# x2 computed token-major in 512-column matmuls and transposed, the last x2 blocks behind the last h, the expert operands in seven tiles built in small pieces

## Chip, cores and metric

The kernel runs on one core of a Trainium2 chip. The metric is the device time of one execution in microseconds (us): the median of several runs.

## The reference

Three layers, one behind the other, on 1536 tokens of 512 values. All arithmetic is float32.

```python
# 1: causal attention in a window of 128, plus 4 sink tokens (2 x 8 heads x 768 x 64)
a = softmax(where(is_sink | in_window, q @ k.T / 8, -1e9)); x = (a @ v) as (1536, 512)
# 2: SoLU layer
h = x @ w_in                                   # 512 -> 1024
solu = h * softmax(h)
ln = (solu - mean) / sqrt(var + 1e-6) * g_ln
x2 = ln @ w_out                                # 1024 -> 512
# 3: 8 experts, all of them for all tokens, weighted by a Sinkhorn-normalised gate
P = exp(x2 @ w_gate - max); 8 times: rows to 1, columns to 1, times N / E
for e in range(8): out += P[:, e] * (relu(x2 @ w1[e]) @ w2[e])
```

## The kernel before

Every float32 product is made of three matmuls on operands split into a high and a low part (`mm3`: high x high, high x low, low x high). A `split` takes one ScalarE copy (high) and one subtract (low), on VectorE from PSUM, or both on GpSimd for weights.

The tokens form T = 12 blocks of 128. A main loop in `fast_path` runs over slots `s`, one for each block and head (NS = 96), and over some more slots until its queues are empty. A slot emits the scores and softmax of one head, the transposes and the a @ v product of earlier heads, the steps of a layer norm that are due (`later`, a table by slot), and then, by `bulk`, a budget of matmuls from a queue: 1.0 us a slot in the first half, 1.3 behind it. The queue holds two kinds of units, written as generators that yield an assumed cost at every matmul:

- `h_unit(t)`: 24 matmuls of 512 columns give h of a block in PSUM (`hp`); behind it come, two to eight slots later, the maximum (L235), exp (L238), the product with its sum (L241), the squares (L249), the norm (L256 and, on GpSimd, L257), and then two groups of four transposes (L268), whose results are split into `lt`. These transposes wait in `tr_q` and are popped at heads 3 and 7, and one a slot behind the last head.
- `x2_unit(p)`: x2 of a pair of blocks, feature-major. The weights `w_out` are the stationary operand, `lt` of the two blocks is the moving one (256 columns): 2 x 48 matmuls into one PSUM bank each (tag `mm`, one buffer). A bank is copied to `x2f` by ScalarE (L310), or, where the pair crosses a boundary of 384 tokens, half by ScalarE (L312) and half by VectorE (L313).

The pairs 0 to 3 are queued with a delay of 28 slots. Pairs 4 and 5 are queued when everything else is done (behind slot NS + 6), after the attention's memory has been closed; then `Experts.begin` is emitted.

The experts take the tokens in four parts of 384 columns, two parts at a time (n = 0, 1), and use seven products instead of eight for each 2 x 2 block product. `build_x(n)` makes the seven operands from `x2f` (X11, X21, X22 and the differences T1 to T4) into one tile of seven parts, 128 x 768 elements a step: a copy on ScalarE (L644), a subtract on VectorE (L645), the differences on VectorE or GpSimd (L649). `begin` builds n = 0; n = 1 is built at the second unit of the experts. The weights of a slice are loaded on SP's queue, combined (L684 to L687) and split (L76, L80) by GpSimd. `Experts.run` goes through 64 units (32 slices x 2), each `first` (7 products of 6 matmuls of 384 columns, L716, with the relu split on L728 and L729) beside `second` of the unit before (36 matmuls of 512 columns). The gate's logits and the Sinkhorn steps go between the products.

The order of instructions on each engine is fixed when the program is built, by a list scheduler that simulates the engines: it takes what is ready in the order of emission, corrected by `high_priority(offset)`, by which instructions move that far forward. Each engine then works through its queue in that order. Memory of a closed pool is used again, and a tile waits for the tiles that lay in its place.

Of the kernel before, what the change touches and what calls it, by code (L numbers as in the profile page):

```python
# [15 lines left out]
P = 128  # L16
# [5 lines left out]
def tile_sink_attention__then__solu_moe__then__sinkhorn_moe(  # L22
# [175 lines left out]
    ln = {}  # L198
# [20 lines left out]
    def h_unit(t, xt, pp, later, tr_q):  # L219

        hp = pp["h"].tile([P, F], F32, name="hp", tag="h")
# [37 lines left out]
        if t % 2 == 0:  # L259
            ln[t // 2] = pp["lnT"].tile([P, 2, KF, 2, P], F32R, name="lt", tag="lt", bufs=2)  # L260
        lt = ln[t // 2]

        def s_tr(g):
# [7 lines left out]
            def post(ps):  # L271
                fs = slice(g * 4, g * 4 + 4)
                split_psum(lt[:, 0, fs, t % 2], lt[:, 1, fs, t % 2], ps)
# [18 lines left out]
    def x2_unit(p, pp):  # L292

        lt = ln.pop(p)
        for b in {2 * p // 3, (2 * p + 1) // 3} - set(x2f):
            x2f[b] = xa_tile(b, [P, KD, NX])
        for d2 in range(KD // 2):
            ps = pp["mm"].tile([P, 2, 2 * P], F32, name="x2p", tag="mm")
            for dd in range(2):
                for f in range(KF):  # L300
                    c0 = (f % 2) * DM + (2 * d2 + dd) * P
                    wt = wout_t[f // 2][:, :, c0:c0 + P]
                    rh, rl = (lt[:, i, f].rearrange("p a b -> p (a b)") for i in range(2))
                    for _ in mm3(ps[:, dd], wt[:, 0], wt[:, 1], rh, rl, f == 0, f == KF - 1):
                        yield 0.109
            ds = slice(2 * d2, 2 * d2 + 2)
            t = 2 * p
            if t % 3 < 2:
                c = t % 3 * P
                nc.scalar.activation(out=x2f[t // 3][:, ds, c:c + 2 * P], in_=ps, func=ACTF.Copy)  # L310
            else:
                nc.scalar.activation(out=x2f[t // 3][:, ds, 2 * P:], in_=ps[:, :, 0:P], func=ACTF.Copy)  # L312
                nc.vector.tensor_copy(x2f[t // 3 + 1][:, ds, 0:P], ps[:, :, P:])  # L313
# [302 lines left out]
    class Experts:  # L616
# [20 lines left out]
        def build_x(self, n, tp):  # L637

            x = self.x[n] = self.xp[n].tile([P, 7, 2, 2, NX], F32R, name=f"x{n}")
# [3 lines left out]
            def put(k, src):  # L643
                nc.scalar.activation(out=x[:, k, 0], in_=src, func=ACTF.Copy)  # L644
                nc.vector.tensor_tensor(out=x[:, k, 1], in0=src, in1=f32(x[:, k, 0]), op=ALU.subtract)  # L645

            def minus(e, z, a, b):
                t = tp(z)
                e.tensor_tensor(out=t, in0=a, in1=b, op=ALU.subtract)  # L649
                return t  # L650

            t3 = minus(nc.gpsimd, 0, b22, b12)
            t1 = minus(nc.vector, 1, b12, b11)
            put(self.X11, b11)
            put(self.T3, t3)
            put(self.X21, b21)
            t2 = minus(nc.vector, 0, b22, t1)
            put(self.T1, t1)
            t4 = minus(nc.gpsimd, 1, b21, t2)
            put(self.T2, t2)  # L660
            put(self.T4, t4)
            put(self.X22, b22)

        def temp(self, tag):
            if tag == "h1":
                return f32(self.hp.tile([P, 2, 2, NX], F32R, name="h1", tag="h1", bufs=2))[:, 0]
            return self.wf.tile([P, 2, NX], F32, name=tag, tag=tag)
# [37 lines left out]
        def seed(self):  # L705

            x = self.x[0][:, 0, 0, 0]
# [3 lines left out]
        def product(self, ps, w, k, x, kx, start):  # L711
            for kk in range(2):
                wh, wl = w[:, 0, k, kk], w[:, 1, k, kk]
                xh, xl = x[:, kx, 0, kk], x[:, kx, 1, kk]
# [75 lines left out]
        def x_parts(self, b):  # L790

            x = self.x[b // 2]
            if b % 2 == 0:
                return x[:, self.X11], x[:, self.X21]
# [93 lines left out]
    def fast_path(stack):  # L888
# [62 lines left out]
        def beside():  # L951

            return tc.high_priority(offset=0)
# [244 lines left out]
```

## Time and profile before

| | |
|---|---|
| median of 3 runs | 1362.11 us (1360.24 to 1362.42) |
| the profiled execution, its own time | 1362.57 us |
| its span, first to last instruction | 1360.5 us |
| mean granted TensorE clock | 0.982 |
| TensorE busy | 1317.5 us (97%) |
| VectorE, GpSimd, ScalarE busy | 708.2, 541.9, 373.4 us |
| chain that ended last | TensorE 89%, VectorE 4% |

Engines are called PE (TensorE), PEld (its weight loads), DVE (VectorE), ACT (ScalarE), POOL (GpSimd) and SP. The granted clock is given as a share: 1.0 is 2.4 GHz, 0.5 is 1.2 GHz. Matmuls overlap, so that the distance of two starts, and not the duration of one, is what a matmul costs in a full queue.

### The profile page before, as it was taken

How to read it: one execution, taken by the hardware profiler on the slowest of the kernel's cores; microseconds unless marked ns; L12 is line 12 of the kernel's file. 1: busy time of each engine (PE TensorE's matmuls, PEld its weight loads, DVE VectorE, ACT ScalarE, POOL GpSimd, SP SyncE). 2: the span in 40 equal slices, each digit the busy share in tenths (PEclk: the TensorE clock that was granted, in tenths of full speed). 3: DMA queues.
4: the chain of work that ended last, by engine and by line, in shares of the span. 5: the costliest groups of instructions: out<-in, count | busy, mean ns of one | idle time of the engine just before them, and what ended most of it. 6: DMA issues, size and time to landing. Idle time of an engine off the chain costs nothing.

```text
span 1360.5 us, 17867 instructions
## 1 busy us (share of the span) xinstructions
PE 1317.5 (97%) x6993; PEld 1171.5 (86%) x6993; DVE 708.2 (52%) x1352; ACT 373.4 (27%) x837; POOL 541.9 (40%) x560
## 2 busy tenths in 40 slices
PE   6799999987999999999999999999999999999998
PEld 5678888886789898989999999989999989999986
DVE  7976554544657454444444444544444544444544
ACT  5666454632422111111111111111111111111111
POOL 7862111243733643444333334444343333334410
PEclk9779999997999999999999999999999999999999
DMA  7411211001101111101111111111111001101102
GB/s 219 136 50 32 47 32 24 9 17 31 47 20 43 32 32 43 36 31 47 32 31 32 32 31 31 32 33 45 32 39 40 32 32 31 32 31 32 32 1 96
DMA packets 86287, 56.38 MB, mean 41 GB/s; under 512 B 41520, under 2 KB 74288, under 8 KB 86192
## 3 DMA queue, kind: packets, MB, share of 16 engines
q1 hardware_dynamic: 86192, 55.13, 13.8%
q8 instruction: 57, 0.93, 0.3%
q14 instruction: 38, 0.31, 0.1%
HBM read 51.97 MB, written 3.15 MB: 41 GB/s over the span
## 4 chain that ended last, share of the span: by engine, by line
PE 89%; DVE 4%; ACT 1%; issue 1%; POOL 0%; DVEq 0%; POOLq 0%; ACTq 0%
PE pb L716 15%; PE p L87 13%; PE p L85 13%; PE p L83 13%; PE pa L716 10%; PE pd L716 5%; PE pz L716 5%; PE av L522 2%; PE x2p L83 2%; PE x2p L85 2%; PE x2p L87 1%; PE hp L87 1%; PE hp L83 1%; PE hp L85 1%; DVE x L645 1%; PE trp L494 1%
## 5 line engine op out<-in xcount | busy, mean ns | idle before, releaser
L783 DVE SCALAR_TENSOR_TENSOR xa<-p,pr,xa 128x512 f32<-128x512 f32 x348 | 250.7, 748 | 207.0 <-PE p L87 207.0
L85 PE MATMUL p<-w,h 128*128 128x512 f32 x768 | 301.3, 392 | 0.0
L83 PE MATMUL p<-w,h 128*128 128x512 f32 x768 | 300.1, 391 | 0.5 <-DVE xa L783 0.5
L87 PE MATMUL p<-w,h 128*128 128x512 f32 x768 | 282.0, 394 | 2.1 <-DVE h L729 2.1
L716 PE MATMUL pb<-x,w 128*128 128x384 f32 x1152 | 234.0, 338 | 0.0
L76 POOL TENSOR_SCALAR w<-wf 128x1792 fp32r<-128x1792 f32 x32 | 54.3, 1697 | 437.2 <-PE pb L716 437.0
L716 PEld LDWEIGHTS pb<-x,w 128*128 128x128 f32 x1152 | 206.0, 188 | 5.7
L87 PEld LDWEIGHTS p<-w,h 128*128 128x128 f32 x768 | 143.6, 188 | 28.7 <-DVE h L729 2.5
L716 PE MATMUL pa<-x,w 128*128 128x384 f32 x768 | 167.1, 340 | 0.2 <-DVE h L729 0.2
L83 PEld LDWEIGHTS p<-w,h 128*128 128x128 f32 x768 | 144.2, 188 | 25.4 <-issue 0.9
L85 PEld LDWEIGHTS p<-w,h 128*128 128x128 f32 x768 | 144.2, 188 | 21.5
L728 ACT ACTIVATE h<-pz 128x384 fp32r<-128x384 f32 x64 | 31.4, 491 | 449.1 <-DVE pz L750 449.1
L716 PEld LDWEIGHTS pa<-x,w 128*128 128x128 f32 x768 | 139.2, 189 | 13.8 <-DVE h L729 0.5
L80 POOL TENSOR_TENSOR w<-wf,w 128x512 fp32r<-128x512 f32 (+1 forms) x128 | 148.3, 1191 | 2.6
L729 DVE SCALAR_TENSOR_TENSOR h<-pb,h 128x384 fp32r<-128x384 f32 x64 | 35.6, 557 | 159.5 <-ACT h L728 159.5
L80 POOL TENSOR_TENSOR w<-wr,w 128x512 fp32r<-128x512 f32 x64 | 83.7, 1330 | 0.2
L728 ACT ACTIVATE h<-pb 128x384 fp32r<-128x384 f32 x64 | 31.5, 492 | 179.1 <-PE pb L716 179.1
L716 PE MATMUL pz<-x,w 128*128 128x384 f32 x384 | 78.0, 338 | 0.0
L716 PE MATMUL pd<-x,w 128*128 128x384 f32 x384 | 77.9, 337 | 0.0
L750 DVE TENSOR_TENSOR pz<-pb,z 128x384 f32<-128x384 f32 x64 | 36.3, 566 | 76.6 <-PE pb L716 76.6
L716 PEld LDWEIGHTS pz<-x,w 128*128 128x128 f32 x384 | 69.2, 188 | 5.3
L83 PE MATMUL x2p<-lt,w 128*128 128x256 f32 x192 | 58.1, 303 | 10.1 <-DVE xa L313 8.9
(203 smaller groups left out, 1899.8 us busy)
## 6 DMA issues: line engine op xcount, KB each, us to landing
wf<-in_moe_w_dram SPq DMA_DIRECT2D x128, 128.0 KB, 2.3
wr<-in_moe_w_dram SPq DMA_DIRECT2D x32, 512.0 KB, 3.5
raw<-in_moe_w_in_dram SPq DMA_DIRECT2D x8, 512.0 KB, 5.9
raw<-in_moe_w_out_dram SPq DMA_DIRECT2D x8, 512.0 KB, 3.6
qk<-in_q_dram SPq DMA_DIRECT2D x12, 256.0 KB, 2.9
qk<-in_k_dram SPq DMA_DIRECT2D x12, 256.0 KB, 2.7
v<-in_v_dram SPq DMA_DIRECT2D x12, 256.0 KB, 2.8
out_dram<-xa SPq DMA_DIRECT2D x12, 256.0 KB, 3.5
```

The costliest lines, as they stand in the source:

```text
L76: nc.gpsimd.tensor_scalar(hi, src, 1.0, 0.0, ALU.mult, ALU.add)
L80: nc.gpsimd.tensor_tensor(lo[:, cs], src[:, cs], f32(hi[:, cs]), ALU.subtract)
L83: nc.tensor.matmul(ps, lhsT=lh, rhs=rh, start=start, stop=False)
L85: nc.tensor.matmul(ps, lhsT=lh, rhs=rl, start=False, stop=False)
L87: nc.tensor.matmul(ps, lhsT=ll, rhs=rh, start=False, stop=stop)
L494: nc.tensor.transpose(ps[:, hh, z], a[:, o:o + P], ident)
L522: nc.tensor.matmul(self.av_ps[:, h], lhsT=at[:, hh, z], rhs=self.raw["v", tv][:, h], start=h == 0 and n == 0, stop=h == H - 1 and n == len ...
L716: nc.tensor.matmul(ps, lhsT=a, rhs=b, start=start and kk == 0 and z == 0, stop=kk == 1 and z == 2, skip_group_check=True,)
L728: nc.scalar.activation(out=h[j][:, f, 0], in_=ps, func=ACTF.Relu)
L729: nc.vector.scalar_tensor_tensor(out=h[j][:, f, 1], in0=ps, scalar=0.0, in1=f32(h[j][:, f, 0]), op0=ALU.max, op1=ALU.subtract)
L750: nc.vector.tensor_tensor(out=pz, in0=pb, in1=z, op=ALU.add)
L783: nc.vector.scalar_tensor_tensor(out=acc, in0=ps, scalar=self.pr[:, t, e:e + 1], in1=acc, op0=ALU.mult, op1=ALU.add)
```

## The change

`x2_unit` now takes one block of 128 tokens, token-major: `lt` is the stationary operand and `w_out` the moving one, 24 matmuls of 512 columns into one bank. ScalarE copies the bank to a staging tile `xs` (one buffer), four TensorE transposes (through `tr_q`, popped at heads 1, 3 and 7) bring it to the feature-major form, and ScalarE copies that to `x2f`. `lt` is a tile per block (four buffers) instead of one per pair (two). A unit may start when its `lt` is written.

The last h unit has PSUM banks of its own (`h2`), and a second bank `mm2` is opened for x2, both in place of the attention's banks. The units of blocks 8 to 11 are queued as soon as the queue has nothing ready behind the last h; from there `begin` is emitted in pieces, two a slot. `beside` moves the slot's own instructions forward by 200 from slot NS - 2 on.

The seven operands of the experts are tiles of their own, and `build_x` is a generator of 22 pieces of 128 x 384 elements; those of n = 1 are emitted two a step in the first two units. The temporary that lay in an h tile is in the pool `lp`. The loop that the general path runs is changed to fit; it isn't executed here.

```diff
-    def h_unit(t, xt, pp, later, tr_q):
+    def h_unit(t, xt, pp, later, tr_q, tag="h"):
-        hp = pp["h"].tile([P, F], F32, name="hp", tag="h")
+        hp = pp[tag].tile([P, F], F32, name="hp", tag=tag)
...
-        if t % 2 == 0:
-            ln[t // 2] = pp["lnT"].tile([P, 2, KF, 2, P], F32R, name="lt", tag="lt", bufs=2)
-        lt = ln[t // 2]
+        lt = pp["lnT"].tile([P, 2, KF, P], F32R, name="lt", tag="lt", bufs=4)
...
+                if g == 1:
+                    ln[t] = lt
...
+    def x2_unit(t, pp, tr_q, tag="mm"):
+        lt = ln.pop(t)
+        b, c = divmod(t, 3)
+        if b not in x2f:
             x2f[b] = xa_tile(b, [P, KD, NX])
+        ps = pp[tag].tile([P, DM], F32, name="x2p", tag=tag)
+        for f in range(KF):
+            cs = slice(f % 2 * DM, f % 2 * DM + DM)
+            wt = wout_t[f // 2]
+            for _ in mm3(ps, lt[:, 0, f], lt[:, 1, f], wt[:, 0, cs], wt[:, 1, cs], f == 0, f == KF - 1):
+                yield 0.227
+        xs = pp["lnT"].tile([P, DM], F32, name="x2s", tag="x2s")
+        nc.scalar.activation(out=xs, in_=ps, func=ACTF.Copy)
+
+        def pe():
+            ps = pp["tr"].tile([P, KD, P], F32, name="trp", tag="tr")
+            for j in range(KD):
+                nc.tensor.transpose(ps[:, j], xs[:, j * P:(j + 1) * P], ident)
+            return ps
+
+        def post(ps):
+            nc.scalar.activation(out=x2f[b][:, :, c * P:(c + 1) * P], in_=ps, func=ACTF.Copy)
+
+        tr_q.append((pe, post))
...
-            x = self.x[n] = self.xp[n].tile([P, 7, 2, 2, NX], F32R, name=f"x{n}")
+            x = self.x[n] = [None] * 7
+            for k in (self.X11, self.T3, self.T1, self.T2, self.X22, self.T4, self.X21):
+                x[k] = self.xp[n].tile([P, 2, 2, NX], F32R, name=f"x{n}_{k}", tag=f"x{n}_{k}")
...
             def put(k, src):
+                for a in range(2):
+                    nc.scalar.activation(out=x[k][:, 0, a], in_=src[:, a], func=ACTF.Copy)
+                    nc.vector.tensor_tensor(
+                        out=x[k][:, 1, a], in0=src[:, a], in1=f32(x[k][:, 0, a]), op=ALU.subtract
+                    )
+                    yield
+            def minus(e, t, a, b):
+                for z in range(2):
+                    e.tensor_tensor(out=t[:, z], in0=a[:, z], in1=b[:, z], op=ALU.subtract)
+                    yield
...
+            build = self.build_x(1, lambda z: self.temp(("tt", "tx")[z]))
             for u, (s, n) in enumerate(units):
-                if u == 1:
-                    self.build_x(1, lambda z: self.temp(("tt", "h1")[z]))
-                if u < 2:
+                if u == 0:
                     step_side()
                     step_side()
...
+                    if u < 2:
+                        next(build, None)
+                        next(build, None)
...
         def begin(self):
-            self.build_x(0, lambda z: self.temp(("tt", "wr")[z]))
             self.load_w1(0)
+            build = self.build_x(0, lambda z: self.temp(("tt", "wr")[z]))
+            for _ in range(4):
+                next(build)
+                yield
             self.split_w1(0)
+            for _ in build:
+                yield
             self.load_w1(1)
             self.load_w2(0)
...
-            return tc.high_priority(offset=0)
+            return tc.high_priority(offset=0 if s < NS - 2 else 200)
+
+        def put_x2(t, tag="mm"):
+            queue.append((lambda: xa and t in ln, x2_unit(t, pp, tr_q, tag)))
...
-                elif tr_q and (h in (3, 7) or s >= NS):
+                elif tr_q and (h in (1, 3, 7) or s >= NS):
...
+                    if tt == T - 1:
+                        psum_a.close()
+                        for nm in ("h", "mm"):
+                            pp[nm + "2"] = pool(psum_b, f"ps_{nm}2", space=PS)
+                    queue.insert(0, (lambda: True, h_unit(tt, fast.x.pop(tt), pp, later, tr_q, "h2" if tt == T - 1 else "h")))
+                    if tt < T - 4:
+                        put_x2(tt)
...
-            if att_open and s > NS + 6 and not queue:
-                att_open = False
+            if begin is None and s > LX + NS - H and not any(x[2:] or x[0]() for x in queue):
                 att.close()
                 ex.open_early(stack)
-                psum_a.close()
-                queue.append((s, x2_unit(T // 2 - 2, pp)))
-                queue.append((s + 10, x2_unit(T // 2 - 1, pp)))
-        ex.begin()
+                for tt in range(T - 4, T):
+                    put_x2(tt, "mm" if tt % 2 else "mm2")
+                begin = ex.begin()
+            if begin:
+                next(begin, None)
+                next(begin, None)
```

## Rows read from the trace of the kernel before

**Rows 1.** Busy time by stretches: us, each engine's busy us (count), granted clock, DMA.

```profile
100.00:300.00 200.00, 199.21 (x1404) 171.67 (x1403) 99.99 (x296) 99.89 (x256) 37.76 (x54) 1.00 0.12 27
300.00:338.00 38.00, 25.39 (x169) 24.11 (x168) 19.59 (x25) 11.00 (x18) 16.51 (x12) 0.82 0.09 28
338.00:377.00 39.00, 36.72 (x192) 31.07 (x191) 23.73 (x26) 17.85 (x34) 26.69 (x17) 0.96 0.14 41
377.00:1345.00 968.00, 967.81 (x4832) 874.22 (x4831) 477.52 (x809) 178.85 (x378) 383.02 (x368) 1.00 0.11 34
```

**Rows 2.** Timeline of TensorE, x2's end: start, us, line, out<-in, count [idle before <-releaser].

```profile
311.42 0.58 PE L83 MATMUL x2p<-lt,w 128*128 128x256 f32 x1 [8.86 <-DVE xa L313]
...
317.13 0.34 PE L87 MATMUL x2p<-lt,w 128*128 128x256 f32 x1
...
322.43 1.09 PE L268 MATMUL trp<-ident,u 128*128 128x128 f32 x8 [2.47 <-POOL u L257]
323.77 0.38 PE L83 MATMUL x2p<-lt,w 128*128 128x256 f32 x1 [0.25 <-ACT lt L67]
324.50 0.58 PE L85 MATMUL x2p<-lt,w 128*128 128x256 f32 x1 [0.34 <-DVE lt L68]
...
327.44 0.31 PE L87 MATMUL x2p<-lt,w 128*128 128x256 f32 x1
...
332.35 0.39 PE L83 MATMUL x2p<-lt,w 128*128 128x256 f32 x1 [0.69 <-ACT xa L310]
...
338.03 0.28 PE L87 MATMUL x2p<-lt,w 128*128 128x256 f32 x1
```

**Rows 3.** Timeline of VectorE, then of ScalarE, in the same stretch.

```profile
303.28 5.35 DVE L645 TENSOR_TENSOR x<-xa,x 128x768 fp32r<-128x768 f32 x3
...
309.75 1.21 DVE L241 CUSTOM_DVE_ANT_0 u<-hp,u 128x1024 f32<-128x1024 f32 x1
...
310.96 0.41 DVE L313 COPY xa<-x2p 128x256 f32<-128x256 f32 x1
...
319.23 0.95 DVE L645 TENSOR_TENSOR x<-wr,x 128x768 fp32r<-128x768 f32 x1
...
313.20 1.12 ACT L249 ACTIVATE hp<-u,st 128x1024 f32<-128x1024 f32 x1 [5.90 <-DVE st L244]
...
331.70 0.60 ACT L310 ACTIVATE xa<-x2p 128x512 f32<-128x512 f32 x1 [7.49 <-PE x2p L87]
```

**Rows 4.** Timelines: last h matmuls of blocks 10, 11; their u on GpSimd.

```profile
282.67 0.39 PE L87 MATMUL hp<-w,xt 128*128 128x512 f32 x1
...
300.70 0.39 PE L87 MATMUL hp<-w,xt 128*128 128x512 f32 x1
...
292.16 2.39 POOL L257 TENSOR_TENSOR u<-u,gains 128x1024 f32<-128x1024 f32 x1 [1.21 <-DVE u L256]
...
319.45 2.92 POOL L257 TENSOR_TENSOR u<-u,gains 128x1024 f32<-128x1024 f32 x1 [0.69 <-DVE u L256]
```

**Rows 5.** Timelines of TensorE, VectorE and GpSimd, start of the experts.

```profile
350.84 0.50 PE L87 MATMUL p<-w,h 128*128 128x512 f32 x1 [2.12 <-DVE h L729]
...
341.84 6.54 DVE L645 TENSOR_TENSOR x<-xa,x 128x768 fp32r<-128x768 f32 x3
...
347.52 6.58 POOL L80 TENSOR_TENSOR w<-wf,w 128x512 fp32r<-128x512 f32 x4
```

**Rows 6.** Timeline of TensorE: one h unit; transposes.

```profile
70.34 0.47 PE L83 MATMUL hp<-w,xt 128*128 128x512 f32 x1
...
75.67 0.39 PE L87 MATMUL hp<-w,xt 128*128 128x512 f32 x1
...
102.15 0.66 PE L268 MATMUL trp<-ident,u 128*128 128x128 f32 x4
...
291.34 0.60 PE L324 MATMUL trp<-ident,xs 128*128 128x128 f32 x4
291.70 0.36 PE L83 MATMUL x2p<-lt,w 128*128 128x256 f32 x1
```

More of the change, by code (lines that the diff above doesn't have):

```diff
@@ L643, in put @@
             def put(k, src):
[L644 to L662, printed above, removed]
+                for a in range(2):
[8 more added lines that the diff above has]
+                    yield
+            t3, t1 = tp(0), tp(1)
+            yield from minus(nc.gpsimd, t3, b22, b12)
+            yield from put(self.X11, b11)
+            yield from minus(nc.vector, t1, b12, b11)
+            yield from put(self.T3, t3)
+            yield from put(self.X21, b21)
+            t2 = tp(0)
+            yield from minus(nc.vector, t2, b22, t1)
+            yield from put(self.T1, t1)
+            yield from put(self.T2, t2)
+            t4 = tp(1)
+            yield from minus(nc.gpsimd, t4, b21, t2)
+            yield from put(self.X22, b22)
+            yield from put(self.T4, t4)
         def temp(self, tag):
-            if tag == "h1":
-                return f32(self.hp.tile([P, 2, 2, NX], F32R, name="h1", tag="h1", bufs=2))[:, 0]
-            return self.wf.tile([P, 2, NX], F32, name=tag, tag=tag)
+            return (self.lp if tag == "tx" else self.wf).tile([P, 2, NX], F32, name=tag, tag=tag)
         def load_w1(self, s):
@@ L705, in seed @@
         def seed(self):
-            x = self.x[0][:, 0, 0, 0]
+            x = self.x[0][self.X11][:, 0, 0]
             for tag in "bd":
@@ L793, in x_parts @@
             if b % 2 == 0:
-                return x[:, self.X11], x[:, self.X21]
+                return x[self.X11], x[self.X21]
             t = self.hp.tile([P, 2, 2, NX], F32R, name="h0", tag="h0", bufs=2)
@@ L936, in bulk @@
             while budget > 0:
-                ready = [x for x in queue if x[0] <= later.slot]
+                ready = [x for x in queue if x[2:] or x[0]()]
                 if not ready:
@@ L940, in bulk @@
                 gen = ready[0]
+                if len(gen) == 2:
+                    queue[queue.index(gen)] = gen = (*gen, True)
                 while budget > 0:
@@ L1024, in fast_path @@
                 if lag == 0 and 0 <= tt < T:
-                    queue.insert(0, (s + 1, h_unit(tt, fast.x.pop(tt), pp, later, tr_q)))
-                    if tt % 2 and tt < T - 4:
-                        queue.append((s + 28, x2_unit(tt // 2, pp)))
+                    if tt == T - 1:
[5 more added lines that the diff above has]
+                        put_x2(tt)
             bulk(1.0 if s < NS // 2 else 1.3)
@@ L1141, in general_path @@
                 later.drain()
-                while tr_q:
+                for g in range(3):
                     pe, post = tr_q.pop(0)
                     post(pe())
-                if t % 2:
-                    for _ in x2_unit(t // 2, pp):
-                        pass
+                    if g == 1:
+                        for _ in x2_unit(t, pp, tr_q):
+                            pass
         wp.close()
@@ L1150, in general_path @@
         ex.open_early(stack)
-        ex.begin()
+        for _ in ex.begin():
+            pass
         ex.open_rest(stack)
```

32 lines of the change are left out of this document (8 added, 24 removed).

## The prediction

> **What bounds the kernel now.** I read the busy time by stretches first, then the idle time in TensorE's order of instructions, then the queues of VectorE, ScalarE and GpSimd where that idle time lies. The stretches [rows 1] split the run in four. From 100 to 300 us (attention, with the h and x2 units filling it) TensorE is busy 199.21 of 200 us, and from 377 to 1345 us (the experts) 967.81 of 968, both at a granted clock of 1.00, the 2.4 GHz level. There only a smaller amount of TensorE work can shorten the run. Between them lie two stretches that are not full: 25.39 of 38 us at clock 0.82, and 36.72 of 39 at 0.96. The first is the end of x2, the second the start of the experts.
>
> TensorE's order shows what is lost in the first [rows 2]. It waits 8.86 us for VectorE's copy of an x2 PSUM bank, then restarts at half clock (27 starts in 5.71 us, 0.21 us apart), waits 2.47 us for the last transposed u, restarts at half clock again, and waits 0.69 us for a ScalarE copy. At full clock the narrow x2 matmuls are (338.03 - 332.35)/47 = 0.121 us apart. So the first restart costs 5.71 - 26 x 0.121 = 2.6 us, and the second (13 steps in 2.94 us) 2.94 - 13 x 0.121 = 1.4 us; 0.6 us more lie in the waits of 0.25 and 0.34 us between. The sum is 8.86 + 2.6 + 2.47 + 1.4 + 0.6 + 0.69 = **16.6 us**.
>
> Why VectorE was late is seen in its queue [rows 3]. The h unit of the last token block ended at 301; VectorE then took the large subtracts of `build_x(0)`, three in 5.35 us, so that the second step of the softmax chain (L241) came at 309.75 and the copy TensorE waited for at 310.96. ScalarE stood 5.90 us in front of the Square, waiting for the same chain. The last block's chain, from the end of its h matmuls to u, took from 301.1 to 322.4 [rows 4]; the block before, undisturbed, took from 283.1 to 294.55, 11.5 us.
>
> In the second stretch TensorE waits 2.12 us for a relu remainder (L729), which stood on VectorE behind subtracts of `build_x(1)`, three of them in 6.54 us [rows 5]. With that, the stretch lost 39 - 36.72 = 2.28 us of idle time, and a mean clock of 0.96 is 2 x 0.04 x 39 = 3.1 us at the 1.2 GHz level, in which half the work, 1.55 us, was lost [rows 1]. Sum **3.8 us**.
>
> **The change part by part.** *Wider matmuls and transposes.* Half an x2 pair was 48 narrow matmuls, 338.03 - 332.35 + 0.12 = 5.80 us [rows 2], twelve times: 69.6 us. A unit is now 24 wide ones; the h unit has the same 24, with activations as weights and 512 columns, and took 75.67 - 70.34 + 0.23 = 5.56 us [rows 6]: 66.7 us. Four transposes took 291.70 - 291.34 = 0.36 us, and the matmul behind them lasted 0.36 us for the usual 0.28, so about 0.09 more [rows 2, 6]: 0.45 x 12 = 5.4 us. Together +2.5 us of TensorE's time, all of which counts, since TensorE is full. Bounds: at 0.119 and 0.227 apart without start costs it is +1.9, with another 0.1 us of switching per group +3.7. I take **+2.5**.
>
> The Trainium skill (TensorE: Matmul & The Clock Gate, Back-to-back issue gap) puts a warm matmul at its columns over 2.4 GHz plus about 2.5 ns. By that 288 wide for 576 narrow saves 0.7 us, where the rows above save 2.9; the sum would be 2.2 us worse.
>
> *Evacuation.* An x2 unit is now copied twice by ScalarE and never by VectorE. That is 24 copies of 512 columns where there were 8 such and 4 half ones; at 0.60 us a copy [rows 3] it adds some 8 us, spread over 12 units. ScalarE is busy 99.89 of 200 us in the filled stretch [rows 1], so it is hidden there; without that cover each costs a wait like the 0.69 us of [rows 2]. The VectorE copy that held TensorE for 8.86 us is gone. The x2 units of blocks 0 to 7 can be emitted from slot 30 instead of 48, but the second half of the first u was transposed only at 102.15 us [rows 6], where TensorE is full already: nothing, at most some tenths.
>
> *Last x2 units behind the last h.* Counting the queue's costs against its budget (1.0 a slot, then 1.3) puts the units of blocks 0 to 7 at slots 32 to 99, the last h at 100 to 103, blocks 8 to 10 at 105 to 116, and block 11 at 117 to 120, behind its transposes at 113 and 114. TensorE takes them somewhat earlier as filler, as it did here. At the end of the last h at least blocks 9 and 10 should be left: 2 x (5.56 + 0.45) = 12.0, plus 0.8 us for eight transposes of the block before; with block 8 it is 18.8 us. Against it stands the chain: 11.5 us as undisturbed, plus transposes and split, about 1.9 (the same steps at 322.43 to 324.50 took 2.07, [rows 2]), 13.4 us. So the uncovered wait is between 0 (18.8 covers 13.4) and, were the chain as slow as now (21.3 + 1.9 = 23.2 against 12.8), 10.4 us plus 1.2 for the clock. The subtracts are half as long and are put between slots, and the chain's steps are ahead of them in priority; each of some five VectorE and GpSimd steps may still find one piece ahead, 0.5 us alone to 1.8 with a GpSimd instruction in front. That is 13.4 + about 4 = 17.4 us against 12.8 to 18.8: I take a wait of **2.0 and 1.2 for the clock**.
>
> *Seven x tiles in pieces.* One tile of 42 KB per partition could be written only when all the memory below it was free; now X11 and T3 can start while TensorE is still in x2. The amount of arithmetic stays: 14 half-size subtracts for 7 (a whole one took 0.95 us without GpSimd's splitting beside it and 1.78 to 2.18 with it, [rows 3, 5]). The Trainium skill (SBUF — State Buffer, Who interferes with whom) says that a VectorE instruction with two SBUF inputs and a GpSimd one that reads SBUF shut each other out for a whole instruction; the 2.18 agrees with 0.95 plus one GpSimd subtract of 1.65 less some overlap. At the start of the experts the pieces go between the products, two per step, so the relu remainder no longer stands behind four subtracts. But `w1` of slice 1 and `w2` of slice 0 are still split by GpSimd only when x2's memory is free; that ended at 347.52 + 6.58 = 354.10, 16 us behind the last x2 matmul [rows 2, 5]. TensorE's work that needs none of it, or `w2` alone, is two logits (16 matmuls) and unit 0 with its second half (42 + 36): 94 at the steady 968/4832 = 0.20 us [rows 1], 18.8 us, just enough. Of the 3.8 us I take **half, 1.9**, as given back; bounds all of it and, were the first products of slice 1 to come 3 us before their weights, a loss of 3.
>
> *Handover.* Behind the last x2 unit stand a ScalarE copy and four transposes before the logits and pz get their PSUM banks; two seed matmuls fit in between. 0 to 2 us, I take **0.9**. The load of `w2` now waits for the last temporary of `build_x(0)`; SP has nothing else queued behind it, and it is needed about 10 us later.
>
> **The sum**: -16.6 + 2.5 + 3.2 - 1.9 + 0.9 = -11.9 us. The profiled execution took 1362.57 us (span 1360.48 and 2.1 around it), 0.46 over the median of 1362.11. 1362.6 - 11.9 = 1350.7; on the scale of the median **1350 us**. A measurement here can't tell less than 0.2% (2.7 us) from no change.
>
> **The rivals.** *Everything is covered*: -16.6 - 3.8 + 2.5 + 0.5 = -17.4, 1345 us. For it: the later slots' chain steps get 200 instructions of priority, so the last h may start earlier than 295 and leave block 8 behind it. Against it: GpSimd has some 16 us of splitting and subtracting in the same window. Chance 0.12.
>
> *The chain is late again*: ScalarE takes instructions in order, and x2's copies now stand in its queue with the Square that waited 5.90 us [rows 3]. If twice as many subtracts each wait for a GpSimd instruction, 14 x (0.5 + 1.65) = 30 us of VectorE queue come for 7 x 2.18 = 15. The wait then is 8 to 10 us instead of 3.2: -16.6 + 2.5 + 9 + 0.9 = -4.2, 1358 us. By the Trainium skill (SBUF — State Buffer, Who interferes with whom) this is what halving does, since the lock goes by instruction. Chance 0.16.
>
> *No change that can be measured*: the same, and the experts' start loses 3 us more for the split weights (16 us against 18.8 is a thin cover): 1361. Chance 0.07.
>
> *Slower*: in the full stretch every x2 unit needs one PSUM bank, one staging tile and a transpose bank, all freed by ScalarE in order, and TensorE's order is fixed. Before, one such wait of 0.69 us is seen at the end [rows 2], and in the full stretch all of TensorE's idle time is 0.8 us [rows 1]. Were each of the 12 units to hold TensorE for 1.7 us (a wait and a restart), 20 us are lost: -11.9 + 20 = +8, 1370 us. It decides from about 1 us a unit. Against it: banks are free for two or more slots before the next unit starts. Chance 0.07.
>
> The forecast itself (1346 to 1355) has 0.58. Faster by over 0.2% is the forecast and the first two, 0.86; same 0.07; slower 0.07. The range 1343.5 to 1359 holds the forecast, the covered case and the late chain.
>
> **What would show it.** x2: 288 matmuls of 512 columns, 0.23 us apart, and 48 transposes at 0.09 to 0.11. The 8.86 us wait gone; a wait of 0 to 4 us in front of the last block's transposes; chain from h to u 12 to 17 us. The last x2 matmul ends at 325 to 330 us instead of 338, and the steady part keeps its 0.20 us a matmul. It is wrong if TensorE shows new waits for ScalarE between 100 and 300 us, if the last chain again takes over 20 us, or if the first products of slice 1 wait for GpSimd.

## The result, and the profile after

The changed kernel took **1383.7 us** (median of 4 runs, 1379.1 to 1386.2), the kernel before 1361.3 in the same comparison: a ratio of 1.015, 95% interval 1.0133 to 1.0168 (the medians are 22.4 us apart). It is slower by about 1.5%, where 1350 was forecast. Its profiled execution took 1385.3 us with a span of 1383.6, 23.1 more than before.

Three marks in TensorE's order divide the loss: the starts of the last h matmul, the last x2 matmul and the last matmul of all. The starts of before are in [rows 2, 4]; its last matmul began at 1354.1. The forecast is split by where its terms belong: two thirds of the wider matmuls to the first line, the other third with the stalls of the tail and the uncovered wait to the second, the expert part and the handover to the third.

| us | before | after | change | forecast |
|---|---|---|---|---|
| to the last h matmul | 300.7 | 322.5 | +21.8 | +1 to +2 |
| from there to the last x2 matmul | 37.3 | 33.4 | -3.9 | about -13 |
| from there to the last matmul | 1016.1 | 1021.2 | +5.2 | -1.0 |

The loss lies mainly where the prediction had put next to nothing. TensorE's order, first in attention, then at the end of x2, then at the start of the experts:

```profile
90.40 0.63 PE L83 MATMUL x2p<-w,lt 128*128 128x512 f32 x1
...
94.34 1.11 PE L266 MATMUL trp<-ident,u 128*128 128x128 f32 x4
...
104.33 0.39 PE L87 MATMUL x2p<-w,lt 128*128 128x512 f32 x1
...
105.81 0.48 PE L83 MATMUL hp<-w,xt 128*128 128x512 f32 x1
...
149.59 0.50 PE L87 MATMUL hp<-w,xt 128*128 128x512 f32 x1 [1.51 <-DVE xt L68]
...
184.01 0.39 PE L85 MATMUL x2p<-w,lt 128*128 128x512 f32 x1
...
187.03 0.40 PE L87 MATMUL x2p<-w,lt 128*128 128x512 f32 x1
...
322.52 0.40 PE L87 MATMUL hp<-w,xt 128*128 128x512 f32 x1
...
333.75 1.11 PE L310 MATMUL trp<-ident,x2s 128*128 128x128 f32 x4 [6.02 <-DVE lt L68]
...
346.94 1.97 PE L266 MATMUL trp<-ident,u 128*128 128x128 f32 x8 [5.51 <-POOL u L257]
...
355.94 0.40 PE L87 MATMUL x2p<-w,lt 128*128 128x512 f32 x1
...
357.95 0.66 PE L310 MATMUL trp<-ident,x2s 128*128 128x128 f32 x4 [1.18 <-ACT x2s L305]
...
367.28 0.89 PE L567 MATMUL lgp<-x,wg_r 128*32 128x384 f32 x4 [1.20 <-ACT lt L572]
372.82 0.50 PE L87 MATMUL p<-w,h 128*128 128x512 f32 x1 [2.57 <-DVE h L739]
...
378.04 1.33 PE L726 MATMUL pb<-x,w 128*128 128x384 f32 x6 [1.12 <-DVE pz L760]
```

The wide x2 matmuls stand 0.232 us apart (13 steps from 184.01 to 187.03), as forecast. But the whole first x2 unit, from 90.40 to 104.33, runs ahead of the h unit of block 2, which starts at 105.81. Before, no x2 matmul stood ahead of that h unit, and it started here:

```profile
95.19 0.57 PE L83 MATMUL hp<-w,xt 128*128 128x512 f32 x1
```

At the end of x2 the wait of 8.86 us of [rows 2] is gone; waits of 6.02, 5.51 and 1.18 us stand there instead. At the start of the experts the wait of 2.12 us of [rows 5] is now 2.57, with two more of 1.2 and 1.1.

VectorE and GpSimd during the last softmax chain, to set beside [rows 3]:

```profile
322.96 1.23 DVE L235 TENSOR_REDUCE st<-hp 128x1 f32<-128x1024 f32 x1 [6.64 <-PE hp L87]
324.10 3.53 DVE L658 TENSOR_TENSOR wr<-xa,xa 128x384 f32<-128x384 f32 x2
327.55 5.55 DVE L651 TENSOR_TENSOR x<-xa,x 128x384 fp32r<-128x384 f32 x6
333.02 0.68 DVE L68 TENSOR_TENSOR lt<-trp,lt 128x512 fp32r<-128x512 f32 x1
...
334.09 1.21 DVE L241 CUSTOM_DVE_ANT_0 u<-hp,u 128x1024 f32<-128x1024 f32 x1
...
325.73 5.55 POOL L80 TENSOR_TENSOR w<-wf,w 128x512 fp32r<-128x512 f32 x4
...
344.55 2.33 POOL L257 TENSOR_TENSOR u<-u,gains 128x1024 f32<-128x1024 f32 x1
```

L241 starts 11.1 us behind L235, though ScalarE had finished the exp at 326: nine half-size pieces of `build_x(0)` stand between them, and eight of these in front of the split of the transposes (L68) for which TensorE waits 6.02 us. From the start of the last h matmul to the transposes of u the chain takes 24.4 us; by the same measure it took 21.7 before [rows 2, 4].

Busy time of each engine and, third from the end, the granted clock in two stretches of attention: of after, then of run e3 below, which has both gates as before, then the first stretch of the kernel before:

```profile
40.00:104.00 64.00, 54.87 (x248) 43.42 (x249) 54.32 (x112) 40.83 (x92) 45.98 (x43) 0.71 0.29 83
104.00:280.00 176.00, 173.95 (x1009) 136.97 (x1008) 86.36 (x250) 88.40 (x223) 26.27 (x42) 0.98 0.13 31
```

```profile
40.00:104.00 64.00, 58.29 (x277) 47.31 (x277) 52.86 (x115) 41.52 (x94) 47.12 (x44) 0.81 0.33 91
104.00:280.00 176.00, 173.03 (x1118) 140.66 (x1117) 96.32 (x289) 99.25 (x258) 30.15 (x47) 1.00 0.13 31
```

```profile
40.00:104.00 64.00, 56.51 (x284) 45.91 (x284) 54.37 (x121) 42.75 (x96) 46.81 (x44) 0.76 0.34 91
```

In the first stretch a clock of 0.71 is 2 x 0.29 x 64 = 37 us at the 1.2 GHz level, against 24 in e3 and 31 before. The second has another 7 us of it, where e3 has none.

### The profile page after: what moved, and what is told of

Read it like the earlier page. It is cut to its first block, busy times and chain, and to the rows that moved or that the text cites. A ratio compares the mean times of both kernels' runs of the same rounds, so it can differ in the third digit from the quotient of the medians.

```text
span 1383.6 us, 17421 instructions
## 1 busy us (share of the span) xinstructions
PE 1333.7 (96%) x6753; PEld 1164.1 (84%) x6753; DVE 719.8 (52%) x1366; ACT 385.4 (28%) x863; POOL 538.8 (39%) x564
## 4 chain that ended last, share of the span: by engine, by line
PE 90%; DVE 3%; POOL 1%; ACT 0%; issue 0%; DVEq 0%; ACTq 0%; POOLq 0%
PE pb L726 14%; PE p L87 13%; PE p L85 13%; PE p L83 13%; PE pa L726 10%; PE pz L726 5%; PE pd L726 5%; PE av L525 2%; PE x2p L83 2%; PE x2p L85 2%; PE x2p L87 1%; DVE x L651 1%; PE hp L87 1%; PE hp L83 1%; PE hp L85 1%; PE trp L497 1%
## 5 line engine op out<-in xcount | busy, mean ns | idle before, releaser
L726 PEld LDWEIGHTS pd<-x,w 128*128 128x128 f32 x384 | 67.9, 188 | 0.1
```

Of the source, the lines that this page charges most:

```text
L726: nc.tensor.matmul(ps, lhsT=a, rhs=b, start=start and kk == 0 and z == 0, stop=kk == 1 and z == 2, skip_group_check=True,)
```

## The experiments

Runs named b edit the kernel before, runs named e the changed one. All were compared with runs of the kernel before on the same chip (medians 1362.3 to 1363.0). "Last h" and "last x2" are starts of matmuls, and the column behind them goes from there to the start of the last matmul of all. "Pairs" counts score matmuls that start less than 0.06 us behind a score matmul of the same line (what that means is told under e12). The counts named in the expectations are up to 4 higher.

| run | median us | ratio, 95% | last h | last x2 | last x2 to last matmul | pairs |
|---|---|---|---|---|---|---|
| before | 1361.3 | | 300.7 | 338.0 | 1016.1 | 82 |
| after | 1383.7 | 1.0133 to 1.0168 | 322.5 | 355.9 | 1021.2 | 70 |
| e1 | 1364.4 | 1.0004 to 1.0027 | 306.6 | 334.9 | 1021.2 | 89 |
| e2 | 1374.7 | 1.0065 to 1.0124 | 313.8 | 344.1 | 1021.9 | 76 |
| e3 | 1358.0 | 0.9952 to 0.9975 | 292.5 | 327.0 | 1022.9 | 107 |
| b1 | 1364.9 | 1.0009 to 1.0032 | 303.5 | 340.9 | 1016.0 | 88 |
| e8 | 1369.1 | 1.0026 to 1.0072 | 309.7 | 339.8 | 1021.2 | 89 |
| b3 | 1352.6 | 0.9907 to 0.9952 | 289.4 | 329.4 | 1015.1 | 107 |
| b6 | 1376.7 | 1.0074 to 1.0135 | 317.8 | 354.7 | 1015.1 | 76 |
| b8 | 1364.6 | 1.0001 to 1.0026 | 304.1 | 342.0 | 1015.1 | 88 |
| b4 | 1370.6 | 1.0042 to 1.0088 | 300.9 | 338.5 | 1023.2 | 82 |
| b5 | 1367.4 | 1.0014 to 1.0046 | 300.6 | 338.0 | 1021.0 | 82 |
| e6 | 1353.8 | 0.9925 to 0.9952 | 292.3 | 326.3 | 1022.8 | 107 |
| e7 | 1357.5 | 0.9957 to 0.9989 | 291.6 | 326.0 | 1022.9 | 107 |
| e10 | 1355.9 | 0.9940 to 0.9979 | 292.2 | 326.6 | 1021.2 | 107 |
| e11 | 1352.4 | 0.9908 to 0.9939 | 292.5 | 326.5 | 1020.8 | 107 |
| e14 | 1353.8 | 0.9905 to 0.9950 | 292.4 | 323.0 | 1020.4 | 107 |
| e12 | 1376.3 | 1.0076 to 1.0135 | 314.1 | 346.9 | 1021.2 | 68 |
| e13 | 1347.8 | 0.9863 to 0.9921 | 291.4 | 319.9 | 1018.8 | 104 |
| e17 | 1345.9 | 0.9846 to 0.9902 | 292.5 | 322.5 | 1015.5 | 104 |

### The two gates: e1, e2, e3, b1

The change lets an h unit be emitted in the slot of its x transposes (before: one slot later), and the x2 units of blocks 0 to 7 as soon as `lt` is written (before: 28 slots behind the h unit of the second block of a pair). e1 takes back the first, e2 the second, e3 both; b1 puts the first alone into the kernel before.

```diff
e1, e3
-queue.insert(0, (lambda: True, h_unit(tt, ...
+queue.insert(0, ((lambda n: lambda: later.slot >= n)(s + 1), h_unit(tt, ...
e2, e3, in put_x2
+due = LX + H * (t | 1) + 28 if t < T - 4 else 0
-queue.append((lambda: xa and t in ln, x2_unit(t, pp, tr_q, tag)))
+queue.append((lambda: xa and t in ln and later.slot >= due, x2_unit(t, pp, tr_q, tag)))
b1
-queue.insert(0, (s + 1, h_unit(tt, ...
+queue.insert(0, (s, h_unit(tt, ...
```

> The changed kernel with one edit undone: an h unit may start only in the slot behind its transposes, as before the change. Theory A (an h unit emitted in the very slot of its transposes stands ahead of the next scores and TensorE waits in it for the split of xt): the early lag goes away, scores of slot 40 come some 8 to 12 us earlier, total about 1372 us. Theory B (x2 units let in from slot 30 lengthen the early slots): no change, 1380 to 1386 us. Theory C (any change of the emission order reshuffles the scheduled order): a change of either sign without this pattern.

> The changed kernel with the x2 units of blocks 0 to 7 held back to the slots from which their pairs were let in before the change. Theory B: the lag of 11 us at slots 32 to 48 goes away and the total is about 1372 us or less. Theory A: the lag stays, 1380 to 1386 us.

> Both edits of the two runs before: h units in the next slot, x2 units in their old slots. If the early order is the whole cause of the lag before 100 us, scores of slot 48 come at about 147 us as before the change, and the total is 1365 to 1372 us (the lag left is four transposes a block and the end of x2). If the lag stays, it is the wide matmuls, the transposes or the scheduler's reshuffling: 1380 us.

> The kernel before with one edit of the change alone: an h unit may start in the slot of its transposes. Theory A: slower than before by 8 to 12 us, 1370 to 1374 us, with the lag at slots 20 to 40. Theory B: same, 1361 us.

The gates are the loss. With both as before (e3) the rest of the change is faster than the kernel before, 1358.0 us. On top of e3 the early x2 costs 6.4 us (e1), the early h unit 16.7 (e2), both 25.7. The same early h unit costs the kernel before only 2.5 us (b1): it must work together with something else in the change. By these times the expectations missed: e1 and e3 came out some 7 us below what they allowed, e2 between its two theories, and b1 far below the 8 to 12 us of its theory A.

What the gates cost TensorE is read from its starts, up to the last x2 matmul: idle time before an instruction is called wait, the rest of the time from one start to the next is called occupied.

| us | occupied | waits | at the 1.2 GHz level | x2 units between the last h matmul and the last u's transposes |
|---|---|---|---|---|
| e3 | 300.5 | 22.5 | 31 | 3.2 |
| e1 (early x2) | 301.0 | 29.9 | 41 | 1.1 |
| e2 (early h unit) | 315.7 | 24.3 | 44 | 3.0 |
| after (both) | 319.8 | 32.3 | 58 | 1.6 |

The two gates cost in different places. Early x2 costs mainly waits: units that ran in attention are missing at the end, where they would have covered the last softmax chain. TensorE's wait for the last u, in e1 and then in e3:

```profile
325.50 1.97 PE L266 MATMUL trp<-ident,u 128*128 128x128 f32 x8 [11.74 <-POOL u L257]
```

```profile
314.28 1.09 PE L266 MATMUL trp<-ident,u 128*128 128x128 f32 x8 [2.75 <-POOL u L257]
```

In after the 6.02 and 5.51 us stand in that place. The early h unit costs occupied time, 15.2 us in e2 and 19.3 in after. Of these 19.3 some 11 are the clock: TensorE works 50 us at the 1.2 GHz level in after and 28 in e3, and half of the difference is lost. The matmuls are the same; the rest is their order (under e12).

### Which pops: e8, b6, b8

With the early h unit, the steps of its chain come a slot earlier, and by the slots of the code the two groups of transposes of u are popped at heads 1 and 3 instead of 3 and 7 (head 1 is a pop that the change added). `lt` is then complete at head 3, and x2 can go ahead of the next h unit, which is queued at head 4. e8 moves the pops of the changed kernel; b6 puts the early h unit into b3 (token-major x2 alone, below), and b8 moves the pops of b6.

```diff
e8, b8
-elif tr_q and (h in (1, 3, 7) or s >= NS):
+elif tr_q and (h in (3, 6, 7) or s >= NS):
b6
-queue.insert(0, (s + 1, h_unit(tt, ...
+queue.insert(0, (s, h_unit(tt, ...
```

> The changed kernel (1383.7 us) with one line changed: transposes waiting in the queue are popped at heads 3, 6 and 7 instead of 1, 3 and 7; the h unit stays in the same slot as its x transposes. Theory A (the earlier h slot hurts only because it brings the chain one slot forward, so that the transposes of u fall on heads 1 and 3, x2 starts before the next h unit is queued, is cut in two by it, and the end of a block is left without filler): the loss goes as with the h unit one slot later, 1360 to 1370 us, and more score matmuls run in pairs than the 71 of the changed kernel. Theory B (the h unit itself, emitted in the slot of its transposes, makes TensorE wait for xt and fall to half clock): 1378 to 1388 us.

> Token-major x2 alone (1352.6 us) with the h unit emitted in the slot of its transposes. Theory A (what makes the early h unit dear are the pops at heads 1, 3 and 7 that token-major x2 brought: the transposes of u come at heads 1 and 3 and x2 starts ahead of the next h unit): 1364 to 1371 us, scores at slot 95 10 us or more later. Theory B (it needs the early x2 units or the new end): 1352 to 1358 us.

> Token-major x2 with the h unit in the slot of its transposes (1376.7 us), the queue of transposes popped at heads 3, 6 and 7 instead of 1, 3 and 7. Theory A (the loss comes through the transposes of u at heads 1 and 3, which let x2 start ahead of the next h unit): most of the 24 us goes, 1353 to 1362 us, with 90 or more pairs of scores. Theory B (it is the h unit's own wait for xt): 1372 to 1378 us.

Token-major x2 with its three pops is enough: the early h unit takes b3 from 1352.6 to 1376.7 us, more than theory A said. Moving the pops gives back 14.6 us of after (e8; e1 gives back 19.3) and 12.2 of the 24 us in b6 (b8, 3 us above its theory A). So a half to three quarters of the early h unit's loss goes through heads 1 and 3. In after, e2 and b6 one whole x2 unit has been issued by the middle of the h unit of block 2, in b3, e1, e3, e8 and b8 half a unit. The other half in b8 was not separated; its clock between 40 and 104 us is 0.76, against 0.81 in b3.

### Token-major x2 alone: b3

The kernel before with the new `x2_unit`, one `lt` per block and the pops at heads 1, 3 and 7. The slots of the x2 units, the end of x2 and the expert part are those of before.

```diff
+ (x2_unit, lt and the pops as in the change)
-queue.append((s + 28, x2_unit(tt // 2, pp)))
+queue += [(s + 28, x2_unit(z, pp, tr_q)) for z in (tt - 1, tt)]
-queue.append((s, x2_unit(T // 2 - 2, pp)))
-queue.append((s + 10, x2_unit(T // 2 - 1, pp)))
+queue += [(s + z // 2 * 10, x2_unit(T - 4 + z, pp, tr_q)) for z in range(4)]
```

> The kernel before (1362 us) with token-major x2 alone: 24 wide matmuls and four transposes a block, in the old slots, the old end (x2 behind everything) and the old build_x. By the prediction's own term it costs 2.5 us of TensorE (1.9 to 3.7), and at the end, where x2 of four blocks stands alone, a copy and four transposes per block that nothing covers, some 2 us: 1364 to 1368 us. Rival (the order of the score matmuls, which run two at a time when they stand side by side, changes with the units beside them): fewer changes of kind with half as many matmuls, 1356 to 1361 us.

1352.6 us, 9.8 less than before: the rival had the right sign, and the gain is larger than it said. Up to the last x2 matmul TensorE's occupied time falls by 3.8 us (x2 matmuls 79.2 to 73.9, transposes 53.7 to 59.0, scores 46.0 to 41.1, the rest up by 1) and its waits fall from 29.7 to 24.8. VectorE no longer copies x2's PSUM banks, and the wait of 8.86 us is gone with it. The clock has a part in this, which the rival did not name: between 40 and 104 us it is 0.81 instead of 0.76. How the gain divides between order and clock was not separated.

### The expert part: b4, b5, e6, e10, e11, e14

b4 is the kernel before with the expert part alone (seven tiles, half-size pieces, n = 1 beside the first two units, T1's temporary in `lp`); b5 the same with whole steps. e6 is e3 with whole steps. e10 is e3 with `build_x(1)` in one go at the second unit; e11 has whole steps besides, and e14 also T1's temporary back in an h tile.

```diff
whole steps (b5, e6, e11, e14)
-for a in range(2):
-    nc.scalar.activation(out=x[k][:, 0, a], in_=src[:, a], func=ACTF.Copy)
-    nc.vector.tensor_tensor(out=x[k][:, 1, a], in0=src[:, a], in1=f32(x[k][:, 0, a]), ...)
-    yield
+nc.scalar.activation(out=x[k][:, 0], in_=src, func=ACTF.Copy)
+nc.vector.tensor_tensor(out=x[k][:, 1], in0=src, in1=f32(x[k][:, 0]), op=ALU.subtract)
+yield
+yield
(and minus() in one step likewise)
one go (e10, e11, e14)
-if u == 0:
+if u == 1:
+    for _ in build:
+        pass
+if u < 2:
     step_side()
     step_side()
...
-        if u < 2:
-            next(build, None)
-            next(build, None)
temporary (e14)
-return (self.lp if tag == "tx" else self.wf).tile([P, 2, NX], F32, name=tag, tag=tag)
+(tag "tx": the first half of an h1 tile)
```

> The kernel before (1362 us) with the expert part of the change alone: seven tiles, build_x in pieces of half size, n = 1 beside the first two units, build_x(0) emitted at one go behind x2. The prediction's term is a gain of 1.9 us, at most 3.8: 1358.5 to 1361.5 us. Theory A of the pieces (they block ScalarE's queue at the start of the experts): from the last x2 matmul to the last matmul 1020 to 1024 us instead of 1016.1, 1366 to 1370 us.

> The kernel before (1362 us) with the expert part of the change alone, as in the run that took 1370.6 us, but with whole steps (128 x 768) of build_x. Theory A (VectorE's subtract and GpSimd's instruction take turns whatever their size, so that halves double the loss; in the run with halves the steps of n = 1 took VectorE 23.5 us against 16.9 in the kernel before, and the first relu remainder came 6.4 us late): 1362 to 1366 us. Theory B (the seven tiles and their order are the loss): 1368 to 1371.

> The both-late version (1358.0 us) with whole steps of build_x (128 x 768) instead of halves, still in seven tiles and still between slots. Theory A (each VectorE subtract waits for one GpSimd instruction, whatever its size, so halving doubles what VectorE loses): the chain from the last h to u falls from 21.8 us to 16 to 19, the start of the experts gets 1 to 3 us shorter, 1353 to 1356 us. Theory B (halves help because a chain step waits for one short piece only): chain 22 to 26 us, 1358 to 1363.

> The both-late version (1358.0 us) in which build_x(1) is emitted in one go at the second unit of the experts, with two steps of the logits ahead of each of the first two units, as the kernel before had it; seven tiles and half-size steps stay. Theory A (pieces emitted beside unit 0 put ScalarE copies that wait for VectorE's differences in front of the copies that free the logits' and products' PSUM banks): from the last x2 matmul to the last matmul 1015 to 1018 us instead of 1022.9, the wait of lgp for ScalarE of 2.9 us goes, 1350 to 1353 us in all. Theory B (the loss at the start of the experts comes from half-size steps that alternate with GpSimd's, whenever they are emitted): no change, 1356 to 1360 us.

> The same with whole steps (128 x 768) of build_x besides. Theory A: 1 to 3 us below the run with half-size steps, 1348 to 1351 us, since VectorE waits for GpSimd half as often in the last chain and at the start of the experts. Theory B (with the order mended, the size of the steps no longer matters): within 1 us of the run with half-size steps.

> The version with build_x(1) in one go and whole steps (1352.4 us), with the temporary T1 of n = 1 back in an h tile as in the kernel before. Theory A (in the memory that is free earlier its subtract and copies go ahead of the logits' copies on ScalarE): from the last x2 matmul to the last matmul 1015 to 1018 us instead of 1020.7, 1347 to 1350 us. Theory B (the start loses to GpSimd's splitting of the second weights): 1351 to 1354 us.

Alone, the expert part costs 8.1 us (b4), nearly all of it behind x2: 1023.2 us instead of 1016.1. TensorE, VectorE and GpSimd in b4:

```profile
343.89 0.54 PE L564 MATMUL lgp<-h,wg_r 128*32 128x384 f32 x2 [1.26 <-ACT lt L569]
...
356.98 0.79 PE L87 MATMUL p<-w,h 128*128 128x512 f32 x1 [6.37 <-DVE h L736]
...
343.06 5.77 DVE L648 TENSOR_TENSOR x<-xa,x 128x384 fp32r<-128x384 f32 x4
348.75 1.64 DVE L648 TENSOR_TENSOR x<-tx,x 128x384 fp32r<-128x384 f32 x1
350.31 3.15 DVE L648 TENSOR_TENSOR x<-xa,x 128x384 fp32r<-128x384 f32 x2
...
342.30 2.98 POOL L655 TENSOR_TENSOR tt<-xa 128x384 f32<-128x384 f32 x2
345.24 3.17 POOL L80 TENSOR_TENSOR w<-wr,w 128x512 fp32r<-128x512 f32 x2
348.37 5.68 POOL L80 TENSOR_TENSOR w<-wf,w 128x512 fp32r<-128x512 f32 x4
```

The relu remainder for which TensorE waited 2.12 us in [rows 5] now costs 6.37, for it stands behind more pieces, and each takes longer. A half-size subtract takes 1.44 us beside a busy GpSimd (5.77 for 4, beside two instructions of 1.49 and two of 1.58 us), and about 1.6 beside GpSimd's splits of 1.42 us each (5.68 for 4). Where GpSimd is idle it takes 0.54, here in e3:

```profile
301.51 0.54 DVE L651 TENSOR_TENSOR x<-tt,x 128x384 fp32r<-128x384 f32 x1
```

A whole one takes 0.95 alone and 2.18 beside GpSimd [rows 3, 5]. Two halves beside GpSimd are therefore 2.9 us for 2.2. Whole steps give back 3.2 us on b4 (b5), 4.2 on e3 (e6) and 3.5 on e10 (e11): of b4's loss halving is about 40%. The last chain gains little by them, 20.9 us in e6 after 21.7 in e3.

The rest is not settled. Emitting n = 1 in one go (e10) took 2.1 us off e3, and not the wait that it was to remove, because ScalarE's queue kept its order:

```profile
335.51 0.52 ACT L650 ACTIVATE x<-tx 128x384 fp32r<-128x384 f32 x1 [4.12 <-DVE tx L658]
337.05 0.52 ACT L650 ACTIVATE x<-tx 128x384 fp32r<-128x384 f32 x1 [1.02 <-DVE tx L658]
...
338.00 0.54 PE L567 MATMUL lgp<-h,wg_r 128*32 128x384 f32 x2 [2.93 <-ACT lt L572]
```

The copy of the logits (L572) that frees their bank stands behind two copies of T1 that wait for VectorE. Putting T1's temporary back in an h tile (e14) left the median where it was, 1353.8 after 1352.4; in e17 below, which differs from e13 by that alone, it goes with 1015.5 us behind x2 after 1018.8. b5 with whole steps still waits 4.77 us for the remainder. By these times b5 lies between its two theories, e10 next to its theory B, and the chain of 16 to 19 us that e6's theory A wanted did not come. The profiled executions of e6 and e11 took 1357.2 and 1356.2 us, 3.4 and 3.8 above the medians, so what is read from their traces need not hold for the medians.

### The last chain: e7

e3 with the loading and splitting of `w1` of slice 0 put behind `build_x(0)`.

```diff
-self.load_w1(0)
 build = self.build_x(0, lambda z: self.temp(("tt", "wr")[z]))
-for _ in range(4):
-    next(build)
-    yield
-self.split_w1(0)
 for _ in build:
     yield
+self.load_w1(0)
+self.split_w1(0)
```

> The both-late version (1358.0 us) with the load and the splitting of w1 of slice 0 put behind build_x(0), as the kernel before had it. Theory A (GpSimd's splitting beside the last softmax chain is what makes its VectorE steps slow): the chain from the last h to u falls from 21.8 us to 13 to 17, the wait of the transposes of u shrinks, and the time is 1352 to 1356 us. Theory B (the splits only move and then hold up the first products): the chain is shorter, but the experts start with a wait of 3 us or more, 1357 to 1362.

Inconclusive: the edit did not move the work. The splitting stayed beside the chain, which took 21.8 us (last h matmul at 291.64, transposes of u at 313.41):

```profile
293.00 5.44 POOL L80 TENSOR_TENSOR w<-wf,w 128x512 fp32r<-128x512 f32 x4
...
313.41 1.09 PE L266 MATMUL trp<-ident,u 128*128 128x128 f32 x8 [2.79 <-POOL u L257]
```

The scheduler put the splits first all the same. Whether the chain would be quicker without them was not tried in another way.

### The order of the scores: e12, e13, e17

The scores of a head use 64 of TensorE's 128 rows. In the trace of after, first a stretch with the scores of two heads side by side, then one head alone; the last line of each is what follows:

```profile
139.32 0.40 PE L83 MATMUL sc<-kh,qT 64*128 64x264 f32 x2
139.54 0.29 PE L85 MATMUL sc<-kl,qT 64*128 64x264 f32 x2
139.67 0.28 PE L87 MATMUL sc<-kh,qT 64*128 64x264 f32 x2
139.88 0.50 PE L532 MATMUL av<-vs,as 96*128 96x512 f32 x1
...
144.38 0.39 PE L83 MATMUL sc<-kh,qT 64*128 64x264 f32 x1
144.61 0.28 PE L85 MATMUL sc<-kl,qT 64*128 64x264 f32 x1
144.73 0.28 PE L87 MATMUL sc<-kh,qT 64*128 64x264 f32 x1
144.94 0.44 PE L497 MATMUL trp<-ident,a 128*128 128x128 f32 x2
```

Six matmuls take 0.56 us, and three alone also take 0.56. A pair that doesn't form costs 0.19 us a matmul. After has 70 pairs and e3 107: 37 x 0.19 = 7 us, about the part of the 19.3 us that the clock leaves. e12 emits two heads' scores together in the changed kernel; e13 does so in e11, and e17 in e14.

```diff
+def scores(self, s):
+    if s % 2 == 0:
+        two = [self.score_mm(s + z) for z in range(2)]
+        (their matmuls in turn, then the maximum of each)
```

> The changed kernel (1383.7 us) with the score matmuls of two heads, which use the two halves of TensorE's rows, emitted side by side in the even slots. Theory A (the changed kernel is slower in attention because fewer scores stand side by side, 71 of 144 possible pairs against 108 in the quick versions, and each single one takes the time of a pair): 130 or more pairs, score matmuls down by 8 to 12 us, 1370 to 1377 us. Theory B (single scores are only filler where TensorE would stand idle): score time falls and waits rise, 1380 to 1388 us.

> The version with build_x(1) in one go and whole steps (1352.4 us), with the scores of two heads emitted side by side. On the changed kernel the same edit left the pairs at 72 and took 7.5 us off, by order and not by pairs. If pairs rise above 108 here, 5 us or more are gained per 30 pairs: 1345 to 1350 us; if not, the edit is a change of order alone and the time may go either way, 1348 to 1358 us.

> The quickest version so far (1347.8 us: both gates as before, build_x in whole steps and n = 1 in one go, scores of two heads emitted side by side) with the temporary of n = 1 in an h tile besides. On the version without the side-by-side scores that temporary made no difference to the median (1353.8 after 1352.4) while the profiled run lost a wait of 4 us: 1345 to 1349 us; if the order falls badly, up to 1352.

As a test of pairs it failed: the scheduler didn't keep the scores side by side (68 pairs in e12, 104 in e13). The edit still took 7.5 us off after and 4.6 off e11. In e12 this goes with the clock: 38 us at the 1.2 GHz level up to the last x2 matmul, 58 in after, with no more pairs. That lost pairs cost the time is therefore read from the trace, not shown by a run. The same reckoning by clock and pairs accounts for 13 of the 15.2 us of occupied time that e2 has over e3, but only for 13 of the 19.7 that b6 has over b3; the rest of b6 is open. e17 is the quickest version found: 1345.9 us, 1.3% below the kernel before (interval 0.9846 to 0.9902); the changed kernel is 2.8% above it.

## Why the prediction was wrong

**Where the time went.** Run by run, the loss is built up so: token-major x2 alone -9.8 us (b3), the new end and the expert part on top +5.4 (e3), the two gates on top +25.7. Together this is +21.3; after stands 20.7 to 22.4 above the medians of before.

**The step that failed** is "Evacuation", where the early x2 units were costed at "nothing, at most some tenths", because the second half of the first u is transposed only at 102.15 us, "where TensorE is full already". Beside it the h unit's gate, a line of the diff, had no term at all. The runs show 25.7 us for the two in place of nothing (after against e3). The 102.15 us did not stand: with the early h unit and the third pop that half is transposed at 94.34, and a whole x2 unit is done at 104.33. And full was read as a store of work that can be taken in any order. The rows that it was read from begin at 100 us; between 40 and 104 us TensorE runs at clock 0.76 before and waits 10 us in all. With the h unit's gate open, a whole x2 unit went ahead of the next h unit, that h unit came 10.6 us later (105.81 for 95.19), and up to 280 us some 14 us more than before went at half clock. With x2's gate open, work that would have covered the last chain was used up before it. By the middle of the last h unit the changed kernel had issued 9.4 x2 units, the one before the work of 8.9: half a unit more, for 21.8 us. Why the early h unit is dear is shown in part only: the pops at heads 1 and 3 carry a half to three quarters of it, and the rest stays open.

**Wider matmuls and transposes (+2.5).** The spacing was right, 0.232 against 0.121 us. The Trainium skill's rule (TensorE: Matmul & The Clock Gate, Back-to-back issue gap), 0.216 us for 512 columns, would have left 2.2 us less gain; the trace, with 0.232, doesn't agree with it. As x2's term it came out at about 0 in b3 (matmuls -5.3, transposes +5.3), there with less time at half clock. What was left out are its side effects, scores -4.9 and waits -4.9.

**The tail (-16.6, wait +3.2).** The long copy wait did go, but -3.9 us came for about -13. The cover was too thin: 1.6 x2 units ran between the last h matmul and the transposes of the last u, fewer than the two of the lower bound. And the chain took 24.4 us where 12 to 17 were forecast: that its steps are ahead of the pieces in priority did not hold, since nine pieces stood between L235 and L241. The rival of the late chain had the wait, 8 to 10 us, for which 6.02 and 5.51 came. Its reason, twice as many subtracts, is at most a small part: whole steps made the chain only 0.8 us shorter (e6), and with 3.2 units of cover the chain of 21.7 us in e3 left a wait of 2.75. Every version here has a chain of 19 to 24 us.

**Seven tiles in pieces (-1.9).** With the handover it came to +5.2 in after, and to +8.1 alone (b4). The bound of +3 rested on late weights; the longest new wait of b4 was for VectorE (6.37 us), and about 40% of its loss is the halving. The rule weighed there (the Trainium skill, SBUF — State Buffer, Who interferes with whom: a VectorE instruction with two SBUF inputs and a GpSimd one that reads SBUF shut each other out for a whole instruction) agrees with the trace, 0.54 against 1.44 us for a half. What halving costs by it was priced for the chain alone, and not for this place.

**Handover (+0.9).** The wait for x2's last copy is 1.18 us, about as forecast.

**The slower rival** had the right sign, and another mechanism: between 100 and 300 us the trace of after shows no wait for x2's copies.

## What to carry to other kernels

A line of a diff that only opens a gate earlier is an edit like any other: write down which work it lets go ahead of which, and look at the stretch where the engine is *not* full, for there the order decided, here over waits and clock. Look also at the stretch that the work is taken from: there it may be missing as cover. Cutting VectorE's two-input instructions in half beside a busy GpSimd made them dearer by a third here (2.9 for 2.2 us). And when a large change moves the time the wrong way, time its parts alone: here the best part (-9.8 us) was hidden under two small ones (+25.7 and +5.4).

## What was not expected of the hardware

Matmuls with 64 rows of two heads ran two at a time when they stood side by side: six in 0.56 us, as long as three alone. The Trainium skill (TensorEngine Tiling (Array Packing), Overview) states up to twice the speed for contractions of 64 or less; the trace agrees with 2.0. With equal work the occupied time up to the end of x2 differed by 6% between e3 and after (300.5 and 319.8 us), clock and order together, and a list of waits does not show this.
